# Splitting four layer-2 loads into 6 KB runs, with the mixer computed in one piece instead of two halves

## The chip, the cores and the metric

The kernel is one program for one core of a Trainium2 chip; the other cores are idle. A core has a matrix engine (PE, with its weight loads shown apart as PEld), a vector engine (DVE), an activation engine (ACT), GpSimd (POOL) and a sync engine (SP), which here only issues transfers. Sixteen DMA engines move data between the chip's memory (HBM) and the core's memory of 128 partitions (SBUF). PE writes its results to a small accumulator memory (PSUM). The metric is the device time in microseconds (us); smaller is better. Every engine runs its own list of instructions in order, and waits on semaphores for the others.

## What is computed

One token passes through two layers of attention over a cache, each followed by a small gated-shift network ("mixer"). All tensors are bf16.

```python
def _A_ref(x, k_cache, v_cache, wq, wo):        # x: 1x1x640; 32 heads of 192; the last 4096 of 32768 cache rows
    q = (x @ wq).reshape(B, Sq, Hq, Dh).transpose(0, 2, 1, 3)
    k, v = k_cache[:, :, Sk - W:, :], v_cache[:, :, Sk - W:, :]
    p = softmax(einsum("bhqd,bhkd->bhqk", q, k) * Dh ** -0.5)
    return einsum("bhqk,bhkd->bhqd", p, v) ... @ wo

def _B_ref(x, w1, w2, w3, w4):                  # one row: every shifted quarter of h is padding, so hs = 0 and x1 = x
    ...
    h2 = gelu(layernorm(x1) @ w3) @ w4          # w3 640x1536, w4 1536x640
    return x1 + h2

x = x + _A_ref(layernorm(x), ...)
x = x + _B_ref(layernorm(x), ...)
x = x + _A_ref(layernorm(x), ...)               # the same weights and caches again
x = x + _B_ref(layernorm(x), ...)
```

With a single row the four shifts of the mixer push the row out and bring zeros in, so `w1` and `w2` have no effect on the result and the kernel does not load them. Each layer reads K and V of 32 heads, 4096 x 192 bf16 = 1.5 MB each, and `wo`; the second layer could reuse the first one's data only as far as SBUF holds it.

## The kernel before

**Memory.** SBUF holds eleven "cells" of 12 KB per partition (`NCELL`, `take`, `give`). Every K, every V, every 960 KB piece of `wo`, most of `w3` and most of `w4` occupies a cell. A cell is popped from the front of the list `free` when the load is written down and appended when its last reader has been written down; a load therefore waits, on SP, for the last reader of the cell's previous content. The activations are kept transposed: 640 values as 128 partitions x 5 columns (`ND` = 5).

**Order of the transfers.** `stream` is one fixed list of all loads of both layers, and SP issues them in that order. A K or V load is a single transfer of 128 partitions x 12,288 contiguous bytes (`load_k` L116, `load_v` L121). Exceptions in `load_v`: the last two heads of a layer come as two transfers of 6,144 bytes per partition each, and of V 3 of layer 2 only the second half is loaded, because the first half is kept in PSUM from layer 1 (`v_words` L438; layer 1 works on its head groups in reverse, so that heads 0 to 6 come last). The transposed K of heads 0 to 6 stay in seven cells from layer 1 to layer 2 (`kept`, `NKEEP`). Layer 2's list begins V 0, V 1, V 2, K 7, the half of V 3, `wo` 0, K 8, V 4, K 9. Their cells come free as follows: V 0's when layer 1's last P V is done, V 1's with the last `wo` piece (L480), V 2's with `w4` (L750), K 7's, V 3's, `wo` 0's, K 8's, V 4's and K 9's when PE has read the kept K of heads 0, 2, 3, 4, 5 and 6 (L370; the cell of head 1 becomes the area for transposed K).

**Attention** (L488). Heads are worked in groups of four. For a K, DVE turns 32x32 blocks (`transpose_quart` L303, L320), PE makes the scores (48 matmuls of a head, L370), ACT the exponentials (L406), PE and DVE the small softmax steps; PV is 32 matmuls of a head (`pv`, L457). `out_proj` (L473) multiplies a group's result with its piece of `wo`, 30 matmuls into `y_ps`; `add_y` adds it to the residual. In the last group `add_y` with n = 0 makes two sums: `x1`, and `z`, the same minus a mean that `center_y` took from the partial sum one group earlier. DVE and ACT add up `z` and its square, so that the mixer's layernorm can start from two sums at once.

**Mixer** (L686). Two one-column matmuls against a matrix of ones spread the sums over the partitions (L692, L694). DVE makes the centred input `xc` (L698) and five small steps for the variance (L703 to L710); ACT takes its logarithm and exponential (`power`, L291). PE multiplies `w3` with `xc` in two halves of six columns (60 matmuls, L722). For each half ACT and DVE evaluate gelu from a square, an exponential and reciprocals (L728 to L741); then 60 matmuls with `w4` (L750), in the order of the halves: 30 that need only the first half's gelu, 30 for the second. Written this way the first half's gelu lies beside the `w3` matmuls of the second half, and the second half's gelu beside the first 30 `w4` matmuls. The end adds the residual (L755, L757), and after the second mixer the result is transposed in bf16 (L771), copied and stored (L774).

The engines PE, DVE, ACT and SP follow the order in which the program is written.

Of the kernel before, what the change touches and what calls it, by code (L numbers as in the profile page):

```python
# [33 lines left out]
def kernel(  # L34
# [39 lines left out]
    VKEEP, VHALF = 3, FREE // 2  # L74

# [39 lines left out]

    def load_k(layer, h):  # L116
        t = take(("k", layer, h))
        nc.sync.dma_start(t[:], A_k_cache[0, h, s0:Sk, :].rearrange("(p j) d -> p (j d)", p=P))
        return t

    def load_v(layer, h):  # L121
        t = take(("v", layer, h))
        src = A_v_cache[0, h, s0:Sk, :].rearrange("(p j) d -> p (j d)", p=P)
        n = 2 if h in GROUPS[layer][-1][-2:] else 1
        step = FREE // n
        if (layer, h) == (1, VKEEP):
            n, step = 2, VHALF
        for i in range(n):
            if (layer, h, i) != (1, VKEEP, 0):
                nc.sync.dma_start(t[:, i * step:(i + 1) * step], src[:, i * step:(i + 1) * step])  # L130
        return t
# [5 lines left out]
    def load_wo(layer, c):  # L137
        t = take(("wo", layer, c))
        src = A_wo[c * QC:(c + 1) * QC, :].rearrange("(p c) n -> p (c n)", c=NA)
        n = 2 if c == GROUPS[layer][-1][0] // QH else 1  # L140
        step = NA * D // n
        for i in range(n):
            nc.sync.dma_start(t[:, i * step:(i + 1) * step], src[:, i * step:(i + 1) * step])
        return t
# [112 lines left out]
    nc.vector.memset(eps1[:], eps)  # L257
    Qblk = const.tile([P, H * NCOL, NM], BF16, name="Qblk")
# [32 lines left out]
    def power(var, mul, bias, tag):  # L291

        ln_t = sm.tile([P, 1], F32, tag=tag + "_ln")
        nc.scalar.activation(ln_t[:], var, ACTF.Ln, bias=bias, scale=mul)
# [192 lines left out]
    def attention(layer, x_cur, rs_cur, x_new, z_new, rs_new, ss_new):  # L487
# [3 lines left out]
        junk = sm.tile([P, ND], F32, tag="ln_junk")  # L491
# [5 lines left out]
        def softmax_scale():  # L497
            rstd = power(total()[:, 0:1], 1.0 / D, eps1[:], "rstd")
# [16 lines left out]
        def add_y(y_ps, n):  # L515
            y_new = x_new if n == 0 else sm.tile([P, ND], F32, name="y_acc")
            if n == 1:

                rs = sm.tile([P, 1], F32, name="rs_y")
                nc.vector.scalar_tensor_tensor(out=y_new[:], in0=y_ps[:], scalar=1.0, in1=y[0][:],  # L520
                                               op0=ALU.mult, op1=ALU.add, accum_out=rs[:, 0:1])

                def center():
                    nm_ps = psm.tile([P, 1], F32, tag="psm")
                    nc.tensor.matmul(nm_ps[:], lhsT=ones[:], rhs=rs[:, 0:1], start=True, stop=True)
                    ym = sm.tile([P, ND], F32, name="y_m")
                    nc.vector.scalar_tensor_tensor(out=ym[:], in0=nm_ps[:, 0:1].broadcast_to([P, ND]),
                                                   scalar=-1.0 / D, in1=y_new[:], op0=ALU.mult, op1=ALU.add)
                    y.append(ym)

                y.append(center)
            else:
                if n == 0:
                    nc.vector.scalar_tensor_tensor(out=z_new[:], in0=y_ps[:], scalar=1.0, in1=y[1][:],
                                                   op0=ALU.mult, op1=ALU.add, accum_out=rs_new[:, 0:1])
                    nc.scalar.activation(junk[:], z_new[:], ACTF.Square, accum_out=ss_new[:, 0:1])
                nc.vector.tensor_add(y_new[:], y[0][:], y_ps[:])  # L537
            y[0] = y_new

        def center_y():  # L540
            y.pop()()
# [26 lines left out]
        for gi, cur in enumerate(groups):  # L568
            nxt = list(enumerate(groups[gi + 1])) if gi + 1 < len(groups) else []
            ST_n = None  # L570
            if nxt:
# [23 lines left out]
                else:  # L595
# [24 lines left out]
                    if pending is not None:  # L620
                        add_y(y_ps, 2)
                        pending = None
# [6 lines left out]
            else:  # L629
                if layer == 0:  # L630
                    add_y(out_proj(layer, *pending), 1)
# [5 lines left out]
            for hq, h in enumerate(cur):  # L637
                o_sb = pv(layer, h, hq, PT, fold)
                if final:
                    if layer == 0 and hq == 1:  # L640
                        center_y()
# [32 lines left out]
            if final:  # L674
                if layer == 1:
                    y_ps = out_proj(layer, *pending)
                    fold()
                    add_y(y_ps, 1)
                    center_y()
                else:  # L680
                    fold()
            pending = (cur[0] // QH, oT)
            ST = ST_n
        add_y(out_proj(layer, *pending), 0)

    def mixer(layer, x_cur, z, rs_cur, ss_cur, x_new, rs_new):  # L686

# [3 lines left out]
        s1_ps = psm.tile([P, 1], F32, tag="psm")  # L691
        nc.tensor.matmul(s1_ps[:], lhsT=ones[:], rhs=rs_cur[:, 0:1], start=True, stop=True)  # L692
        s2_ps = psm.tile([P, 1], F32, tag="psm")
        nc.tensor.matmul(s2_ps[:], lhsT=ones[:], rhs=ss_cur[:, 0:1], start=True, stop=True)  # L694
        xc = sm.tile([P, ND], BF16, name="xc")
        xcf = sm.tile([P, ND], F32, name="xcf")
        for t in (xc, xcf):
            nc.vector.scalar_tensor_tensor(out=t[:], in0=s1_ps[:, 0:1].broadcast_to([P, ND]), scalar=-1.0 / D,  # L698
                                           in1=z[:], op0=ALU.mult, op1=ALU.add)

        st = sm.tile([P, 4], F32, name="st")
        m2, s2d, b1, b2 = (st[:, i:i + 1] for i in range(4))
        nc.vector.tensor_scalar(out=b1, in0=s1_ps[:], scalar1=1.0 / D, scalar2=None, op0=ALU.mult)  # L703
        nc.vector.tensor_tensor(out=m2, in0=b1, in1=b1, op=ALU.mult)
        nc.vector.tensor_scalar(out=b2, in0=m2, scalar1=-(1.0 + eps), scalar2=eps * eps, op0=ALU.mult, op1=ALU.add)
        nc.vector.scalar_tensor_tensor(out=s2d, in0=s2_ps[:], scalar=1.0 / D, in1=m2, op0=ALU.mult, op1=ALU.max)
        rr = power(s2d, 1.0 + eps, b2, "rr")
        rg = sm.tile([P, 1], F32, name="rg")
        nc.vector.tensor_scalar(out=rg[:], in0=rr[:], scalar1=GELU_A * GELU_C, scalar2=None, op0=ALU.mult)
        nc.vector.tensor_scalar(out=b1, in0=m2, scalar1=-1.0, scalar2=eps, op0=ALU.mult, op1=ALU.add)  # L710

        HF = NF // 2
        hT = sm.tile([P, NF], BF16, name="hT")
        h_ps = []
        for half in range(2):
            hp = psS.tile([P, 4, NGK, NM], F32, name="ST_ps")
            hp = hp[:, 0].rearrange("p g m -> p (g m)")[:, 0:HF]
            for i in range(HF):
                fc = half * HF + i
                f0 = 2 * P * (fc // 2) + fc % 2  # L720
                for kc in range(ND):
                    nc.tensor.matmul(  # L722
                        hp[:, i:i + 1], lhsT=w3[kc][:, f0:f0 + 2 * P - 1:2], rhs=xc[:, kc:kc + 1],
                        start=(kc == 0), stop=(kc == ND - 1))
            h_ps.append(hp)
        for half, hp in enumerate(h_ps):
            sq = sm.tile([P, HF], F32, name="sq")
            nc.scalar.activation(sq[:], hp, ACTF.Square, scale=rr[:, 0:1])  # L728
            gu = sm.tile([P, HF], F32, name="gu")
            nc.vector.scalar_tensor_tensor(out=gu[:], in0=sq[:], scalar=1.0 / GELU_C, in1=hp,  # L730
                                           op0=ALU.add, op1=ALU.mult)
            ge = sm.tile([P, HF], F32, name="ge")
            nc.scalar.activation(ge[:], gu[:], ACTF.Exp, scale=rg[:, 0:1])

            rh = sm.tile([P, HF], F32, name="rh")
            nc.vector.tensor_scalar(out=rh[:], in0=hp, scalar1=rr[:, 0:1], scalar2=None, op0=ALU.mult)
            nc.vector.reciprocal(rh[:], rh[:])
            nc.vector.scalar_tensor_tensor(out=gu[:], in0=ge[:], scalar=1.0, in1=rh[:],
                                           op0=ALU.add, op1=ALU.mult)
            with nc.allow_low_precision(reason="the matmul's operand, bf16 as in the reference"):  # L740
                nc.vector.reciprocal(hT[:, half * HF:(half + 1) * HF], gu[:])  # L741
        rstd = power(s2d, 1.0, b1, "rstd")
# [5 lines left out]
        order = [(n, half * HF + i) for half in range(2) for n in range(ND) for i in range(HF)]  # L748
        for i, (n, fc) in enumerate(order):
            nc.tensor.matmul(  # L750
                y2_ps[:, n:n + 1], lhsT=w4[fc][:, n * P:(n + 1) * P], rhs=hT[:, fc:fc + 1],
                start=(i == 0), stop=(i == len(order) - 1))
# [9 lines left out]
    rs2 = const.tile([P, 1], F32, name="rs2")  # L762
    z = [const.tile([P, ND], F32, name=f"z{i}") for i in range(2)]
    zs = [const.tile([P, 1], F32, name=f"zs{i}") for i in range(4)]
    attention(0, xT, rs0, x1, z[0], zs[0], zs[1])
    mixer(0, x1, z[0], zs[0], zs[1], x2, rs2)
    attention(1, x2, rs2, x3, z[1], zs[2], zs[3])
    mixer(1, x3, z[1], zs[2], zs[3], x4, None)

# [35 lines left out]
```

## Time and profile before

| | us |
|---|---|
| median of three runs (range) | 537.08 (536.6 to 537.44) |
| the profiled execution | 537.44 |
| its span in the profile | 536.3 |
| PE / PEld / DVE / ACT busy | 282.2 / 230.1 / 260.4 / 55.7 |
| packets of the kernel's transfers, share of 16 DMA engines' span | 97.8% |
| last 480 KB piece of `wo` issued to landed | 15.9 |

The profile's span is one execution as the hardware recorded it; what lies around it, 1.1 us, is start and end of the launch. "GB/s" in a row of stages is what all sixteen DMA engines moved; outside the start, the end and one stretch after layer 1 it is about 424. In the chain of work that ended last, 71% of the span are transfers, and a piece called "issue" is time in which an engine waited for nothing that the profile shows. The transfers named "instruction" are the engines' own program code. A matmul on this page is shown with 165 ns and more, but successive ones overlap: 48 score matmuls with their weight loads take 1.37 us.

### The profile page before, as it was taken

The numbers are of one execution on the slowest core, as the hardware profiler recorded it, in microseconds if no ns is written. First come the engines' busy times: TensorE is split into PE (matmuls) and PEld (weight loads), VectorE is DVE, ScalarE is ACT, GpSimd is POOL, SyncE is SP. The second block draws the span as 40 slices with busy tenths as digits, with TensorE's granted clock in tenths as the row PEclk, the third lists the DMA queues.
The fourth block names the chain that finished last, engine by engine and source line by source line (L and its number), as shares of the span: only waits on it lengthen the run. The fifth ranks groups of instructions, "written<-read, shape, count | busy, mean of one in ns | idle before, by whom it ended". The sixth has DMA issues, their size and how long they took to land.

```text
span 536.3 us, 14902 instructions
## 1 busy us (share of the span) xinstructions
PE 282.2 (53%) x6824; PEld 230.1 (43%) x6824; DVE 260.4 (49%) x519; ACT 55.7 (10%) x253; POOL 2.0 (0%) x11
## 2 busy tenths in 40 slices
PE   0046555365363654545545686666364554536555
PEld 0045444253352543434434664554253443425445
DVE  2187546455455555455414137665454653645612
ACT  1001010010100101001202012010010101001021
POOL 1000000000000000000000000000000000000000
PEclk9999999999999999999999996555555555555555
DMA  8999999999999999999999999999999999999993
GB/s 343 432 426 423 418 427 423 423 425 421 423 422 423 421 424 423 423 424 422 399 404 409 355 369 425 422 424 421 427 420 423 424 420 425 425 423 423 424 412 131
DMA packets 23698, 219.48 MB, mean 409 GB/s; under 512 B 2516, under 2 KB 2900, under 8 KB 8148
## 3 DMA queue, kind: packets, MB, share of 16 engines
q1 hardware_dynamic: 23636, 218.54, 97.8%
q8 instruction: 53, 0.87, 0.7%
q14 instruction: 9, 0.07, 0.0%
HBM read 218.53 MB, written 0.00 MB: 407 GB/s over the span
## 4 chain that ended last, share of the span: by engine, by line
DMA 71%; PE 14%; DVE 12%; issue 2%; ACT 1%; SPq 0%; DVEq 0%
DVE cell_4835 L320 6%; DMA cell_570<-in_A_k_cache_dram 6%; DMA cell_1056<-in_A_k_cache_dram 5%; DMA cell_1668<-in_A_v_cache_dram 5%; DMA cell_2032<-in_A_k_cache_dram 5%; DMA cell_2520<-in_A_k_cache_dram 5%; DMA cell_3009<-in_A_k_cache_dram 5%; DMA cell_7450<-in_A_k_cache_dram 5%; DMA cell_5986<-in_A_k_cache_dram 5%; DMA cell_7943<-in_A_v_cache_dram 5%; DMA cell_6474<-in_A_k_cache_dram 5%; DMA cell_6962<-in_A_k_cache_dram 5%; PE O_ps L457 4%; DMA cell_3469<-in_A_k_cache_dram 4%; PE ST_ps L370 3%; DMA cell_8141<-in_A_wo_dram 3%
## 5 line engine op out<-in xcount | busy, mean ns | idle before, releaser
L370 PE MATMUL ST_ps<-Qblk,cell_203 128*128 128x4 bf16 x1200 | 45.7, 168 | 72.2 <-DVE cell_203 L320 72.2
L370 PE MATMUL ST_ps<-Qblk,cell_4835 128*128 128x4 bf16 x1200 | 45.5, 168 | 64.4 <-DVE cell_4835 L320 63.8
L461 DVE STREAM_TRANSPOSE o_sb<-O_ps 128x192 f32<-128x192 f32 x64 | 24.5, 382 | 112.8 <-PE O_ps L457 112.8
L457 PEld LDWEIGHTS <-PT 128*1 128x1 bf16 x2048 | 68.2, 115 | 22.7 <-issue 11.5
L370 PEld LDWEIGHTS <-cell_203 128*128 128x128 bf16 x1200 | 38.6, 105 | 85.1 <-DVE cell_203 L320 83.4
L370 PEld LDWEIGHTS <-cell_4835 128*128 128x128 bf16 x1200 | 38.6, 105 | 78.1 <-DVE cell_4835 L320 75.3
L470 ACT ACTIVATE oT<-oT_ps,rl 32x6 bf16<-32x6 f32 x64 | 16.5, 257 | 282.4 <-PE oT_ps L469 282.4
L406 ACT ACTIVATE Pr<-ST_ps,nb_sb,sc 128x32 bf16<-128x32 f32 x64 | 25.1, 489 | 0.5
L337 PE MATMUL qT_ps<-xc,wq_sb 128*128 128x1 bf16 x480 | 15.9, 166 | 13.5 <-DMA wq_sb<-in_A_wq_dram 13.0
L469 PE MATMUL oT_ps<-o_sb,Lq 128*32 128x6 f32 x128 | 16.9, 204 | 11.4 <-DVE o_sb L461 11.2
L337 PEld LDWEIGHTS <-wq_sb 128*128 128x128 bf16 x480 | 15.0, 105 | 14.2 <-DMA wq_sb<-in_A_wq_dram 13.7
L469 PEld LDWEIGHTS oT_ps<-o_sb,Lq 128*32 128x32 f32 x128 | 11.9, 141 | 19.8 <-issue 15.3
L415 PEld LDWEIGHTS <-Eq 128*32 128x32 bf16 x256 | 4.0, 105 | 30.9 <-DVE y_acc L537 25.1
L351 PE MATMUL Qrep_ps<-Xq,Lb 128*128 128x24 bf16 (+1 forms) x18 | 3.2, 180 | 24.4 <-DVE Xq L344 24.2
L406 ACT ACTIVATION_READ_ACCUMULATOR Pr<-ST_ps,nb_sb,sc 128x1 f32 x64 | 14.4, 226 | 0.0
L402 ACT COPY nb_sb<-nb_ps 128x4 f32<-128x4 f32 x16 | 2.6, 162 | 113.1 <-PE nb_ps L400 113.1
L344 DVE TENSOR_TENSOR Xq<-qT_ps,maskq 128x24 bf16<-128x24 f32 (+1 forms) x18 | 2.8, 155 | 19.6 <-PE qT_ps L337 19.5
L420 PE MATMUL l_ps<-lpart,ones 128*128 128x4 f32 x32 | 9.5, 366 | 5.3 <-ACT PT L418 5.3
L420 PEld LDWEIGHTS l_ps<-lpart,ones 128*128 128x128 f32 x32 | 8.1, 313 | 6.9 <-ACT PT L418 6.7
L400 PE MATMUL nb_ps<-dg,ones 4*128 4x4 f32 x32 | 9.0, 348 | 1.0
L400 PEld LDWEIGHTS nb_ps<-dg,ones 4*128 4x128 f32 x32 | 7.9, 307 | 1.8
L415 PE MATMUL PT_ps<-Pr,Eq 128*32 128x32 bf16 x256 | 5.3, 192 | 6.0 <-ACT Pr L406 5.8
(285 smaller groups left out, 476.2 us busy)
## 6 DMA issues: line engine op xcount, KB each, us to landing
wq_sb<-in_A_wq_dram SPq DMA_DIRECT2D x5, 1536.0 KB, 11.2
cell_201<-in_A_k_cache_dram SPq DMA_DIRECT2D x1, 1536.0 KB, 21.9
cell_259<-in_A_k_cache_dram SPq DMA_DIRECT2D x1, 1536.0 KB, 25.1
cell_320<-in_A_k_cache_dram SPq DMA_DIRECT2D x1, 1536.0 KB, 25.8
cell_374<-in_A_k_cache_dram SPq DMA_DIRECT2D x1, 1536.0 KB
cell_465<-in_A_k_cache_dram SPq DMA_DIRECT2D x1, 1536.0 KB, 30.3
cell_568<-in_A_v_cache_dram SPq DMA_DIRECT2D x1, 1536.0 KB, 30.3
cell_570<-in_A_k_cache_dram SPq DMA_DIRECT2D x1, 1536.0 KB, 30.3
```

Source lines behind the costliest of these rows:

```text
L320: nc.vector.transpose(Tu, Ku[:, :, q * NY:(q + 1) * NY])
L337: nc.tensor.matmul(qT_ps[:, tl:tl + 1], lhsT=wq_sb[:, kc, t * P:(t + 1) * P], rhs=xc[:, kc:kc + 1], start=(kc == 0), stop=(kc == ND - 1))
L351: nc.tensor.matmul(Qrep_ps[:], lhsT=Lb[:], rhs=held["x"][:].rearrange("p t b -> p (t b)"), start=True, stop=True)
L370: nc.tensor.matmul(ST_ps[:, hq, q * ng + g, :], lhsT=T4[:, g, f, :, t], rhs=Qblk[:, h * NCOL + 2 * f + t, :], start=(n == 0), stop=(n == N ...
L400: nc.tensor.matmul(nb_ps[:], lhsT=ones[0:n, :], rhs=held["dg"][0:n, :], start=True, stop=True)
L406: nc.scalar.activation(out=Pr[:, hq].rearrange("p m g -> p g m"), in_=ST_ps[:, hq], func=ACTF.Exp, bias=nb_sb[:, hq:hq + 1], scale=sc[:, 0 ...
L415: nc.tensor.matmul(PT_ps[32 * m:32 * (m + 1), :, j, :], lhsT=Eq[:, j, :], rhs=held["Pr"][:, :, m, :], start=True, stop=True)
L420: nc.tensor.matmul(l_ps[:], lhsT=ones[:], rhs=held["l"][:], start=True, stop=True)
L457: nc.tensor.matmul(O_ps[r:r + 1, :], lhsT=PT[:, hq, i:i + 1], rhs=V[:, i * Dh:(i + 1) * Dh], start=(i < 4), stop=(i >= NB - 4))
L461: nc.vector.transpose(o_sb[:], O_ps[:].rearrange("p (a c) -> p c a", c=NA))
L469: nc.tensor.matmul(oT_ps[r, :], lhsT=Lq[:], rhs=o_sb[:, :, 0], start=True, stop=True)
L470: nc.scalar.activation(oT[r, :], oT_ps[r, :], ACTF.Copy, scale=rl[r, 0:1])
```

## The change

Two parts are put in place of one another.

Loads: `parts(layer, h)` returns 2 for layer 2 (`layer == 1`) and heads 1, 2 and 7 (`SHORT`), else 1, and `load_k`, `load_v` and `load_wo` issue that many transfers, each over all 128 partitions and 6,144 bytes of each. So V 1, V 2 and K 7 of layer 2 are issued as two transfers each; as the test is on the head's number alone, V 7 is too. K 1 and K 2 are not loaded in layer 2, and `load_wo` asks with multiples of four, which `SHORT` does not hold. Layer 2 issues four transfers more, of the same bytes in total.

Mixer: it works in one piece. `center_y`, `z`, the two sums and the five small variance steps are gone. `add_y` makes the new residual and its row sum; `ln_center`, the function that attention uses already, spreads the mean by one matmul, makes `xc` and `xcf` and sums the squares on ACT; the variance is spread by a matmul (`total`) that stands on PE behind the first 25 of the 60 `w3` matmuls. Gelu runs once on all twelve columns, behind the last `w3` matmul, and `w4` follows it, output column by output column. The result is transposed in bf16, as before.

```diff
+    SHORT = (1, 2, 7)
...
+    def parts(layer, h):
+
+        return 2 if layer == 1 and h in SHORT else 1
+
     def load_k(layer, h):
         t = take(("k", layer, h))
-        nc.sync.dma_start(t[:], A_k_cache[0, h, s0:Sk, :].rearrange("(p j) d -> p (j d)", p=P))
+        src = A_k_cache[0, h, s0:Sk, :].rearrange("(p j) d -> p (j d)", p=P)
+        n = parts(layer, h)
+        step = FREE // n
+        for i in range(n):
+            nc.sync.dma_start(t[:, i * step:(i + 1) * step], src[:, i * step:(i + 1) * step])
...
-        n = 2 if h in GROUPS[layer][-1][-2:] else 1
+        n = 2 if h in GROUPS[layer][-1][-2:] else parts(layer, h)
...
-        n = 2 if c == GROUPS[layer][-1][0] // QH else 1
+        n = 2 if c == GROUPS[layer][-1][0] // QH else parts(layer, c * QH)
...
-            if n == 1:
-                rs = sm.tile([P, 1], F32, name="rs_y")
-                nc.vector.scalar_tensor_tensor(out=y_new[:], in0=y_ps[:], scalar=1.0, in1=y[0][:],
-                                               op0=ALU.mult, op1=ALU.add, accum_out=rs[:, 0:1])
-                def center():
-                    nm_ps = psm.tile([P, 1], F32, tag="psm")
-                    nc.tensor.matmul(nm_ps[:], lhsT=ones[:], rhs=rs[:, 0:1], start=True, stop=True)
...
+        def add_y(y_ps, last):
+            if last:
+                nc.vector.scalar_tensor_tensor(out=x_new[:], in0=y_ps[:], scalar=1.0, in1=y[0][:],
+                                               op0=ALU.mult, op1=ALU.add, accum_out=rs_new[:, 0:1])
+                return
...
+    def mixer(layer, x_cur, rs_cur, x_new, rs_new):
         w3 = need("w3", 0)
-        s1_ps = psm.tile([P, 1], F32, tag="psm")
-        nc.tensor.matmul(s1_ps[:], lhsT=ones[:], rhs=rs_cur[:, 0:1], start=True, stop=True)
-        s2_ps = psm.tile([P, 1], F32, tag="psm")
-        nc.tensor.matmul(s2_ps[:], lhsT=ones[:], rhs=ss_cur[:, 0:1], start=True, stop=True)
...
-        for half in range(2):
-            hp = psS.tile([P, 4, NGK, NM], F32, name="ST_ps")
...
+        xc, xcf, total = ln_center(x_cur, rs_cur)
+        hT_ps = psm.tile([P, NF], F32, tag="psm")
+        for fc in range(NF):
+            f0 = 2 * P * (fc // 2) + fc % 2
+            for kc in range(ND):
+                nc.tensor.matmul(
+                    hT_ps[:, fc:fc + 1], lhsT=w3[kc][:, f0:f0 + 2 * P - 1:2], rhs=xc[:, kc:kc + 1],
+                    start=(kc == 0), stop=(kc == ND - 1))
+            if fc == NF // 3:
+                var_ps = total()
+                rr = power(var_ps, 1.0 + eps, eps2, "rr")
...
+        nc.scalar.activation(sq[:], hT_ps[:], ACTF.Square, scale=rr[:, 0:1])
...
+        nc.scalar.activation(ge[:], gu[:], ACTF.Exp, scale=rg[:, 0:1])
...
+            nc.vector.reciprocal(hT[:], gu[:])
...
-        order = [(n, half * HF + i) for half in range(2) for n in range(ND) for i in range(HF)]
...
+        for n in range(ND):
+            for fc in range(NF):
+                nc.tensor.matmul(
+                    y2_ps[:, n:n + 1], lhsT=w4[fc][:, n * P:(n + 1) * P], rhs=hT[:, fc:fc + 1],
+                    start=(fc == 0), stop=(fc == NF - 1))
```

## The prediction, made before the run

> **What bounds the kernel.** The page comes first: which engine is full, and what the chain that ended last is made of.
>
> ```profile
> PE 282.2 (53%) x6824; PEld 230.1 (43%) x6824; DVE 260.4 (49%) x519; ACT 55.7 (10%) x253; POOL 2.0 (0%) x11
> ...
> q1 hardware_dynamic: 23636, 218.54, 97.8%
> q8 instruction: 53, 0.87, 0.7%
> ...
> DMA 71%; PE 14%; DVE 12%; issue 2%; ACT 1%; SPq 0%; DVEq 0%
> ```
>
> No engine is full; the transfers are. 218.5 MB at 424 GB/s are 515 us of 536.3. A change can save only where the transfers are not at that rate, and at the end, after the last of them. Rows by stage find these places (times, busy us with counts, granted clock, DMA share, GB/s last):
>
> ```profile
> 286.00:299.00 13.00, 8.45 (x228) 8.06 (x229) 4.29 (x31) 2.76 (x13) 0.00 (x0) 1.00 1.03 415
> 299.00:316.00 17.00, 13.70 (x421) 12.62 (x418) 2.26 (x13) 2.47 (x12) 0.00 (x0) 1.00 0.89 326
> 316.00:358.00 42.00, 27.64 (x670) 22.26 (x671) 27.41 (x47) 5.45 (x26) 0.00 (x0) 0.63 1.01 424
> 358.00:511.00 153.00, 80.07 (x1920) 64.75 (x1918) 80.65 (x139) 14.52 (x67) 0.00 (x0) 0.50 1.01 423
> ```
>
> From 299 to 316, the start of layer 2, the rate is 326: 17 x (1 - 326/424) = 3.9 us of transfer time are lost. The timeline of SP shows why: a load goes out only when its cell is free.
>
> ```profile
> 288.17 0.33 SPq L130 DMA_DIRECT2D cell_4829<-in_A_v_cache_dram  x1
> 293.52 0.33 SPq L130 DMA_DIRECT2D cell_4831<-in_A_v_cache_dram  x1
> 299.45 0.33 SPq L118 DMA_DIRECT2D cell_4833<-in_A_k_cache_dram  x1
> 304.39 0.33 SPq L130 DMA_DIRECT2D cell_4962<-in_A_v_cache_dram  x1
> 307.82 0.33 SPq L143 DMA_DIRECT2D cell_5008<-in_A_wo_dram  x1
> 309.11 0.33 SPq L118 DMA_DIRECT2D cell_5010<-in_A_k_cache_dram  x1
> ```
>
> These are V 1, V 2, K 7, half of V 3, `wo` 0 and K 8, freed by PE. What holds PE there is in the chain in order of time:
>
> ```profile
> 293.52 1.86 issue
> 295.38 0.23 PE y_ps L750 x2
> ...
> 300.59 0.99 issue
> 301.58 0.27 PE ST_ps L370 x4
> ...
> 305.53 1.97 issue
> 307.50 1.58 PE ST_ps L370 x53
> ```
>
> Three times PE stands still with nothing to wait for: 4.8 us. I counted PE's instructions up to each stop: 6,849, 7,105 and 7,361, 256 apart. The 53 packets of the queue "instruction" have 16,384 bytes each; PE has 13,705 instructions, so a packet is a block of 256. PE runs out of program. The packet records say when a block came: fetches start at 293.00, 299.10 and 305.17, move for 1.0 us, and PE goes on 1.3 to 1.4 us after their ends. All through the trace a fetch starts after PE has entered the block before it. From that entry to its start it takes 1.9 to 3.7 us in most of the span, about 3.0, while 12,288-byte packets (median 462 ns) fill the engines; at the three stops 5.2, 3.7 and 3.6. Two started with mostly 6,144-byte packets around them (236 ns): 0.9 us at 272.98 and 1.4 at 308.87; one with the queues nearly empty, 0.6 at 529.85. I read it so: the fetch waits behind data packets, and shorter packets shorten the wait.
>
> **The change, part by part.** The sum is made against the profiled 537.44, which is 0.36 above the median of the runs.
>
> *Mixer, second layer: all on the path, after the last transfer.* Before, the first `w3` matmul starts at 528.70 and the last `w4` matmul ends at 533.35: 4.65 us. After: 60 `w3` matmuls 1.74 (528.70 to 530.44); the variance matmul between them 0.45 (distance of the two spreading matmuls); gelu once, from its square to the first `w4` matmul 1.37 as in the first half at 290.37 to 291.74, and 0.05 to reach ACT; 60 `w4` matmuls 1.75. Sum 5.36: +0.7. From below +0.25, if the variance matmul hides; from above +1.05, as in the second mixer DVE waited another 0.33 before L738. What precedes `xc` is as long as before (one vector step, one spreading matmul). I take +0.75. `rr` is no bound: the variance is there 25 x 0.029 + 0.6 = 1.3 us after the first matmul, its logarithm and exponential take 0.55, and `w3` ends at 2.2.
>
> *Mixer, first layer.* The same arithmetic puts the last `w4` matmul near 294.6 instead of 293.5. But the block boundary (6,849) now falls just behind that matmul, since the program before it is nearly equally long: PE computes on to the end of `w4` while the block is fetched. The fetch began at 293.00, behind V 0, which is not split; so the block comes at 295.38 as before, and the next layer's mean matmul starts at about 295.4 instead of 295.86. The 1.1 us is hidden by that wait; without the wait it would be +1.1. V 2 goes out 0.9 us later, at 294.4; V 1 keeps the engines until 296.7, so it is not missed. What queues behind V 2 on SP, K 7, waits for PE until 299 anyway.
>
> *Split loads, the rate.* 16 x 236 ns instead of 8 x 462 per engine are +0.08 us a transfer; by the means (242, 468) +0.13. Four transfers: +0.3 to +0.5; I take +0.45. Four more issues of 0.33 us on SP lie in its waits of several us between the issues shown; were that cover gone, +1.3.
>
> Does a smaller transfer cost more in itself? Layer 2's last V heads go in halves of 768 KB, and the row for 514 to 516, mostly theirs, has 419 GB/s:
>
> ```profile
> 514.00:516.00 2.00, 1.51 (x42) 1.17 (x34) 0.38 (x1) 0.26 (x1) 0.00 (x0) 0.50 1.02 419
> 502.00:508.00 6.00, 4.05 (x93) 3.03 (x97) 2.86 (x6) 0.51 (x2) 0.00 (x0) 0.50 1.00 420
> ```
>
> The Trainium skill speaks against the change here: "DMA: Bandwidth & Descriptors", section "Rules for kernel authors", asks for 1 MiB per transfer or more, and its section on the anatomy of one DMA, told for GpSimd's path, has a fixed 2.0 us for each; by that, four more would be an estimated +8 us and the kernel near 543. The rows show this cost overlapped while others are queued.
>
> *Split loads, the fetches.* Fetch 2 is asked for at 295.4, with V 1's second half and V 2 in the engines, fetch 3 with V 2 and K 7. Wait with 6 KB runs: from below 0.9, from above 3.7 as it was; nearest are the two rows with 6,144-byte packets; as those engines were less full I take 2.0. Then fetch 2 starts at 297.4, its block is there at 299.8, and PE needs it at 300.4 - 0.45 = 299.95: the second stop is gone. Fetch 3: 299.95 + 2.0 + 2.4 = 304.35, needed at 303.7: 0.6 instead of 2.0. The next, at 308.7 against 308.5, may cost 0.2. So PE is ahead by 0.45, then 1.5, then 3.1 us. V 3 goes out at 302.8, `wo` 0 at 304.7, K 8 at 306.0.
>
> The Trainium skill, same page, section "Queues, rings and completion order", has an engine drain a packet of some 9 to 17 descriptors of one ring before it turns to another. By it a fetch would wait for up to 8 x 0.462 = 3.7 us, and 1.9 with 6 KB runs; the 5.2 us at the first stop is beyond that.
>
> *What the transfers gain.* A first packet follows its issue by about 1.05 us here. Taking the engines as one server at 424 GB/s (3.7 us for 1.5 MB), before: V 2 done 300.4, K 7 starts 300.95, is done 304.65, V 3 starts 305.6, is done 307.45, `wo` starts 309.0, V 4 is done 318.7: 3.05 idle. After: K 7 (issued 299.0) starts 300.4, and nothing is idle behind it; V 4 is done 3.0 earlier. From above: the 3.9 us of the stage row, less 0.5 that remains. From below 0, if PE gains nothing; a loss is excluded here, since a shorter packet ahead gives a fetch no longer wait. I take 3.0. From 316 the rate is 424 and the queue stays deep (14 to 30 us from issue to landing), so what is gained there arrives at the end. Late next is nothing until 358, where PE waits for transfers again.
>
> Sum: -3.0 + 0.45 + 0.75 = -1.8; 535.6 against the profiled execution, 535.3 against the median.
>
> **Rivals.**
>
> *Fetches do not shorten (slower).* If the wait is set by something else than run length, fetch 2 takes 3.7 us from 295.38 again, the block comes at 301.5 as before, and the 0.45 is lost too. Gain 0, +0.45 + 0.75: 538.3. For it: only two rows with 6 KB, and the engines were not full in either. Against: the wait follows what is in the engines, from 0.6 to 5.2. It decides from where fetches 2 and 3 together save less than 0.75 us of their 7.3.
>
> *Part of the gain.* One stop stays, because the third fetch falls behind a skewed engine or V 3 and `wo` are short of a full queue anyway: a gain of 1.5 to 2 is 536.3 to 536.8. The engines do end their transfers up to 3 us apart.
>
> *More.* V 1's halves also shorten the first fetch (its record starts when V 0's 128 packets have just been started, so V 0 seems to set it). At 291.5 the first stop is gone, the mean matmul starts at 295.0, and with 3.9 recovered the sum is -2.7 to -3.2: 534.2.
>
> **How the numbers follow.** A measurement of this kernel tells 0.2%, 1.1 us, from no change: faster is below 536.0, slower above 538.2. The forecast, with its own range of 534.4 (gain 3.4, tail +0.25) to 536.2 (gain 2.4, tail +1.05): 0.60, of which 0.06 lies above 536.0. Part of the gain: 0.14, of which 0.02 is faster. More: 0.10. No shortening: 0.16; 538.3 is just beyond the bound, and a longer tail puts it further, so 0.11 is slower. Faster 0.54 + 0.02 + 0.10 = 0.66; same 0.06 + 0.12 + 0.05 = 0.23; slower 0.11. The range leaves out some of "more" and most of "no shortening", 0.2 in all: 533.9 to 537.6.
>
> **What will show it.** In the chain of the changed kernel, between the end of layer 1 and 320 us: an "issue" piece of some 0.5 us right before the mean matmul (L284), none or one under 0.7 at the scores. PE's 6,849th instruction stays at about 295.4. `wo` 0 of layer 2 issued near 304.7. The stage 299 to 316 above 380 GB/s. From the last `wo` matmul to the store +0.75 us. The prediction is wrong if the stops stand as they were, if the stage's rate rises and a later stage's falls by as much, or if the rate of the split transfers themselves is under 400.

## The result

The changed kernel takes 540.97 us (median; 540.07 to 541.9) against 537.26 us on the same measure: 1.007 times the time before, with a 95% interval of 1.0049 to 1.0091. It is slower, by 0.7%. A second comparison on another occasion, below, gave 1.0046 (1.0030 to 1.0062). The ratios here are those on record; they are formed from all the executions and differ a little from the ratio of the two medians. The forecast was 535.3 and faster; the range ended at 537.6.

The profiled execution after has a span of 538.9 us, 2.6 more than before. The chain of work that ended last, in order of time, around the start of layer 2 (start, duration, what):

```profile
293.50 1.75 PE y_ps L712 x60
295.28 0.18 DVE x_138 L719 x2
295.46 0.57 issue
296.03 0.57 PE mean_ps L284 x2
...
300.76 1.44 issue
302.19 0.22 PE ST_ps L381 x3
...
306.12 2.27 issue
308.39 1.53 PE ST_ps L381 x52
```

The first stop is as foretold, a piece of half a microsecond right before the mean matmul. The second and the third, which were to vanish and to shrink to 0.6, are 1.44 and 2.27 us; before they were 0.99 and 1.97. SP's issues show what follows from that (a pair is now one line, x2):

```profile
288.61 0.81 SPq L139 DMA_DIRECT2D cell_4803<-in_A_v_cache_dram  x2
295.19 0.80 SPq L139 DMA_DIRECT2D cell_4806<-in_A_v_cache_dram  x2
299.59 1.65 SPq L127 DMA_DIRECT2D cell_4809<-in_A_k_cache_dram  x2
304.95 0.33 SPq L139 DMA_DIRECT2D cell_4939<-in_A_v_cache_dram  x1
308.67 0.33 SPq L152 DMA_DIRECT2D cell_4985<-in_A_wo_dram  x1
309.95 0.33 SPq L127 DMA_DIRECT2D cell_4987<-in_A_k_cache_dram  x1
```

`wo` 0 goes out at 308.67, not at 304.7, and the stage of 299 to 316 us keeps the rate that it had (times, busy us with counts, granted clock, DMA share, GB/s last):

```profile
286.00:299.00 13.00, 8.56 (x235) 7.83 (x224) 2.85 (x20) 2.25 (x11) 0.00 (x0) 1.00 1.00 390
299.00:316.00 17.00, 13.01 (x414) 12.43 (x415) 2.38 (x12) 2.47 (x12) 0.00 (x0) 1.00 0.91 326
```

The end, from the last piece of `wo` to the transposed result, is the chain's last part:

```profile
512.45 16.23 DMA cell_8114<-in_A_wo_dram
528.68 0.05 issue
...
530.39 0.80 PE hT_ps L680 x25
531.20 0.43 PE var_ps L297 x2
531.62 0.95 PE hT_ps L680 x35
...
532.65 0.28 ACT sq L689
...
534.21 1.75 PE y_ps L712 x60
...
536.20 0.28 PE row_ps L731
```

In the kernel before, the same part of the chain begins and ends so:

```profile
511.04 15.91 DMA cell_8141<-in_A_wo_dram
...
533.60 0.28 PE row_ps L771
```

From the landing at 528.68 to the transposing matmul at 536.20 it is 7.52 us; before it was 526.95 to 533.60, 6.65. That is +0.9. The rest of the 2.6 us is already there when `wo` lands: 528.68 against 526.95, 1.7 us late. Much of this came about where nothing was changed. Two long stretches in which the transfers alone set the time, one of them in layer 1, ran at 423 GB/s before:

```profile
20.00:250.00 230.00, 119.28 (x2896) 97.35 (x2896) 124.88 (x213) 20.91 (x97) 0.00 (x0) 1.00 1.01 423
340.00:500.00 160.00, 84.83 (x2059) 69.19 (x2060) 87.11 (x147) 15.14 (x70) 0.00 (x0) 0.50 1.01 423
```

and after:

```profile
20.00:250.00 230.00, 119.11 (x2896) 97.27 (x2896) 124.50 (x213) 20.91 (x97) 0.00 (x0) 1.00 1.01 422
340.00:500.00 160.00, 85.05 (x2067) 69.08 (x2056) 86.36 (x147) 15.16 (x70) 0.00 (x0) 1.00 1.01 422
```

The records of the single packets resolve this better. From 20 to 250 us a 12,288-byte packet took 465.6 ns in the mean before and 467.2 after. By the starts of the packets, the way from 4 to 118 MB took 271.65 us before and 272.23 after, that from 136 to 216 MB 190.22 and 190.77: +1.1 us together. No step of the prediction has this. Between the two, around the start of layer 2, the way from 118 to 136 MB took 46.95 and 47.64, +0.7; but from one profiled execution to another it lay anywhere between 45.9 and 48.5 with the old mixer and between 46.9 and 48.0 with the new one, so nothing follows from that difference.

### The profile page after: what moved, and what is told of

Same layout as the page of the kernel before. It is cut to its first block, busy times and chain, and to the rows that moved or that the text cites. A ratio compares the mean times of both kernels' runs of the same rounds, so it can differ in the third digit from the quotient of the medians.

```text
span 538.9 us, 14872 instructions
## 1 busy us (share of the span) xinstructions
PE 281.8 (52%) x6820; PEld 229.0 (42%) x6820; DVE 257.4 (48%) x494; ACT 54.7 (10%) x249; POOL 2.0 (0%) x11
## 4 chain that ended last, share of the span: by engine, by line
DMA 70%; PE 15%; DVE 11%; issue 2%; ACT 1%; SPq 0%; DVEq 0%; ACTq 0%
DVE cell_4812 L331 6%; DMA cell_567<-in_A_k_cache_dram 6%; DMA cell_1665<-in_A_v_cache_dram 5%; DMA cell_1053<-in_A_k_cache_dram 5%; DMA cell_2029<-in_A_k_cache_dram 5%; DMA cell_2517<-in_A_k_cache_dram 5%; DMA cell_3006<-in_A_k_cache_dram 5%; DMA cell_7428<-in_A_k_cache_dram 5%; DMA cell_7921<-in_A_v_cache_dram 5%; DMA cell_5964<-in_A_k_cache_dram 5%; DMA cell_6940<-in_A_k_cache_dram 5%; DMA cell_6452<-in_A_k_cache_dram 5%; PE O_ps L468 4%; DMA cell_3466<-in_A_k_cache_dram 4%; PE ST_ps L381 3%; DMA cell_8114<-in_A_wo_dram 3%
```

## Experiments

### Which of the two parts

The load part alone on the kernel before (`load_k` and `load_v` with it, as in the change):

```diff
+    SHORT = (1, 2, 7)
...
+    def parts(layer, h):
+
+        return 2 if layer == 1 and h in SHORT else 1
```

> Only the loads are split; the mixer stays in halves. Theory A (the mixer in one piece costs the time, the split nothing but slightly slower packets): within +0.2 to +0.7 us of the kernel before. Theory B (the split costs most of the 3.7 us): +2 us or more. Both expect the three issue stops of PE at the start of layer 2 as long as before, 4.5 to 5.5 us together, since in the changed kernel the waits of the program fetches did not shorten; had run length mattered, they would be under 2 us together and the time 534 to 535.

The mixer part alone (the changed kernel with no load split):

```diff
-    SHORT = (1, 2, 7)
+    SHORT = ()
```

> Only the mixer is in one piece; no load of layer 2 is split but those that were before. Theory A: +2 to +3.2 us, made of about +0.9 at the end (last wo piece landed to the store) and of V 2 issued 1.2 us or more later behind w4, so that the rate of the stage 286 to 299 falls from 415 to about 390 GB/s. Theory B: +0.9 at the end and at most +0.3 elsewhere, about +1.1 in all.

The changed kernel as it is, on the same measure:

> The changed kernel once more, on the chip of the other three, as the sum that the two parts have to make: +2.6 to +4.5 us against the kernel before. If the parts add up, it is split_only plus mixer_only within 0.7 us.

Measured against 538.77 us for the kernel before: the split alone 538.19, ratio 0.9992 (0.9977 to 1.0006); the mixer alone 540.38, 1.0042 (1.0027 to 1.0057); both 540.84, 1.0046 (1.0030 to 1.0062). The whole loss comes with the kernel that has the new mixer; the split neither gains nor costs anything that can be measured. The tail, from the landing of `wo`'s last piece to the transposing matmul, is 7.52 or 7.53 us in all five profiled kernels with the mixer in one piece and 6.63 to 6.67 in the nine with halves and no split load. In the two with halves and split loads it is 6.29 and 6.30, as the wait of 0.33 us that DVE had before L738 is missing there; why, no run shows.

### What sets a program fetch's wait

Layer 2's V 0 takes the other of two free cells, so that it is issued later:

```diff
+        if (layer, h) == (1, 0):
+            free[0], free[1] = free[1], free[0]
```

> The kernel before, but V 0 and V 1 of layer 2 change cells: V 0 now waits for the last wo piece's cell, and is issued near 288.2 instead of 286.0, after PE has asked for its next block of program (287.8); V 1 follows at once. Theory Q (a fetch waits for what was issued before it): the fetch that began at 293.0 begins at 289.5 to 291.5 when w4's rest is done, the first stop of 1.9 us is gone or under 0.5, K 7 goes out 1.4 to 1.9 us earlier (near 297.8), and the time falls by 0.8 to 1.8 us, to 535.5 to 536.5. Theory R (a fetch waits some fixed time whenever the engines are full, whatever was issued before it): it begins at 292 to 293.5, the stop stays at 1.3 us or more, the time is within 0.5 us of before, or slower by up to 0.5 since V 0 starts late.

The dose of the split doubled, to runs of 3 KB (against the run with the split alone, so with the mixer in halves):

```diff
-        return 2 if layer == 1 and h in SHORT else 1
+        return 4 if layer == 1 and h in SHORT else 1
```

> The kernel before with V 1, V 2 and K 7 of layer 2 issued as four transfers of 3 KB runs each, in place of one of 12 KB. It doubles the dose of the split. If the length of the runs ahead of a program fetch sets its wait (the prediction's step on the fetches), the waits of the 26th to 28th fetch fall from 5.2, 3.7 and 3.6 us to about 1 to 1.5 and the stops of 0.99 and 1.97 us go. If the bytes ahead set it, as the half-sized transfers and the run with a quarter of V 1 and V 2 speak for, the waits stay at 3.5 to 5 us and the stops stand. The time: unchanged, or up to 0.8 us longer, since 3,072-byte packets took 121 ns, which is 484 for 12 KB against 466, over 7.1 MB.

Fewer bytes instead of shorter runs:

```diff
+        if layer == 1 and h in (1, 2):
+            n, step = 1, FREE // 4
...
+        k = (lambda i: i % 8) if layer == 1 and h in (1, 2) else (lambda i: i)
...
-            nc.tensor.matmul(O_ps[r:r + 1, :], lhsT=PT[:, hq, i:i + 1], rhs=V[:, i * Dh:(i + 1) * Dh],
+            nc.tensor.matmul(O_ps[r:r + 1, :], lhsT=PT[:, hq, i:i + 1], rhs=V[:, k(i) * Dh:(k(i) + 1) * Dh],
```

> The kernel before, but of V 1 and V 2 of layer 2 only the first quarter is loaded and used over and over (three quarters of their sums over the cache are left out): 2.4 MB less, 5.6 us of transfer less. It shows what the second program fetch of the mixer's stretch waits for, asked for at 295.4. Theory Q (it waits for data in the engines): these are nearly empty by then, it starts within 1.5 us instead of 3.7, and the second stop of 1.0 us is gone. Theory R (the wait is the fetch's own): it starts 3 us or more after it was asked for and the stop stays. Theory Q also expects the third stop of 2.0 us to shrink, as only K 7 is then under way; the time falls by 5.6 us at most, less where the queue is empty anyway.

From the packet records of the program's queue: the time from PE's entry into a block to the start of the fetch of the next one, for the 26th, 27th and 28th fetch (those behind the three stops).

| kernel | runs of V 1, V 2, K 7 | waits, us |
|---|---|---|
| before | 12 KB | 5.2, 3.7, 3.6 |
| V 0 late | 12 KB | 5.2, 3.7, 4.0 |
| mixer alone | 12 KB | 3.5, 3.9, 3.8 |
| split alone | 6 KB | 5.0, 3.8, 4.2 |
| changed kernel | 6 KB | 5.1, 3.9, 3.7 |
| changed kernel again | 6 KB | 3.5, 3.5, 3.7 |
| split in four | 3 KB | 5.3, 3.7, 3.8 |
| a quarter of V 1 and V 2 | 12 KB of K 7; V 1 and V 2 3 KB | 5.1, 1.1, 2.9 |

The stops in the chain of the kernel split in four:

```profile
293.51 2.18 issue
...
300.90 0.99 issue
...
305.84 2.25 issue
```

and in the chain of the one with a quarter of V 1 and V 2, where the second stop is gone:

```profile
293.49 1.91 issue
...
304.39 1.19 issue
```

In this last one the stage before the missing stop moved only 276 GB/s:

```profile
286.00:299.00 13.00, 8.42 (x228) 8.01 (x229) 4.26 (x31) 2.76 (x13) 0.00 (x0) 1.00 0.73 276
```

A fourfold cut of the run length left the second and third wait at 3.7 and 3.8, so the length of the runs does not set the wait. A cut of the bytes brought the second to 1.1, so the data beside a fetch do have a part in it.

The two rows with short packets, from which the prediction took its 2.0 us, were not of one kind. By the packet records of the kernel before, the engines were busy for 61% of the time in which the fetch of 308.87 waited; they were running empty. But while the fetch of 272.98 waited they were busy for 96%, with packets of 6,144 and 3,072 bytes, and that fetch waited only 0.5 to 1.1 us in all sixteen profiles, with the engines at 89% or more. So full engines alone do not make a wait long, and less full ones do not always make it short: in the changed kernel's second profile they were 84% busy during the second wait, and it was 3.5 us. What sets the wait stays open. The trace of the kernel before held two more rows on run length: the fetch that started at 510.98 waited 2.9 us, with 6,144-byte packets for 29% of the engines' busy time, and the one that started at 522.05 waited 3.1 with full engines and no packet over 7,680 bytes around it. Neither is clearly shorter than the usual 3.0.

The Trainium skill, "DMA: Bandwidth & Descriptors", section "Queues, rings and completion order", has an engine drain a packet of some 9 to 17 descriptors before it turns to another ring; by that, as an estimate, a fetch would have waited half as long behind 6 KB runs and a quarter as long behind 3 KB, which is not what was measured.

The times: V 0 late 538.13 against 538.77 (0.9994, 0.9977 to 1.0011), split in four 538.21 against 538.42 (0.9999, 0.9985 to 1.0012); the quarter 535.44 in a single run, with 2.4 MB less to load. With V 0 issued at 288.47, after the fetch had been asked for at 288.14, the first fetch waited 5.2 us all the same; so it does not wait only for what was issued ahead of it. Whether V 0 sets that wait, as the prediction had supposed, is not settled by this: before and with V 0 late, 123 and 107 packets of 12,288 bytes started between the asking and the fetch. Why the first wait is 5.1 in some executions and 3.5 in others, of the changed kernel too, stays open.

### Where the slower packets come from

What differs between the two kernels in layer 1, up to its last head groups, is the place of the cells. The constants lie ahead of them in SBUF, each small tile taking 32 bytes. The new mixer has six of them fewer (z0, z1, zs0 to zs3) and three more (eps2, rs1, rs3), so the cells begin at byte 89,568 instead of 89,664. A cell is 12,288 bytes, 48 x 256, so all eleven cells have the same place relative to 256 bytes. The first three runs moved them by widening or joining constants.

The kernel before with its cells at 89,696:

```diff
-    eps1 = const.tile([P, 1], F32, name="eps1")
+    eps1 = const.tile([P, 16], F32, name="eps1")[:, 0:1]
```

> The kernel before with one constant made 32 bytes larger, so that all eleven cells begin 32 bytes later: at 89,696 instead of 89,664 bytes of each partition, no longer a multiple of 64, as in the changed kernel (89,568). Nothing else differs. Theory C (the cells' place makes every packet slower): the median 12,288-byte packet takes 464 ns instead of 462, and the time rises by 0.6 to 1.6 us. Theory D (the slower packets of the changed kernel come from the chip or the day): 462 ns, time within 0.4 us of before.

The changed kernel with its cells at 89,600, a multiple of 512:

```diff
-    eps2 = const.tile([P, 1], F32, name="eps2")
+    eps2 = const.tile([P, 16], F32, name="eps2")[:, 0:1]
```

> The changed kernel with one constant made 32 bytes larger, so that the cells begin at 89,600, a multiple of 64 again. Theory C: the packets take 462 ns again and 0.6 to 1.6 us of the changed kernel's loss are gone, so +0.8 to +1.9 us against the kernel before; what stays is the tail of the mixer in one piece, +0.9 to +1.2 between the last wo piece's landing and the store. Theory D: as the changed kernel, +2.1 to +3.7.

The kernel before with its cells at 89,600:

```diff
-    even = const.tile([P, 1], F32, name="even")
+    evlo = const.tile([P, 2], F32, name="evlo")
+    even, lo = evlo[:, 0:1], evlo[:, 1:2]
...
-    lo = const.tile([P, 1], F32, name="lo")
...
-    maskq = const.tile([P, 4], F32, name="maskq")
+    mb = const.tile([P, 8], F32, name="mb")
+    maskq, blkm = mb[:, 0:4], mb[:, 4:8]
...
-    blkm = const.tile([P, NM], F32, name="blkm")
```

> The kernel before with four small constants merged into two, so that the cells begin at 89,600, a multiple of 512, instead of 89,664, a multiple of 64 alone. Theory C1 (only the 64 matters): within 0.4 us of the kernel before, packets 462 ns. Theory C2 (a wider alignment gives more): 460 ns or less and 0.5 us or more faster.

Against 538.43 us: the kernel before moved by 32 bytes 537.64 (0.9987, 0.9974 to 1.0000), so 32 bytes as such do no harm; the changed kernel at 89,600 533.85 (0.9919, 0.9895 to 0.9943); the kernel before at 89,600 **532.81 (0.9897, 0.9876 to 0.9918)**, faster than both kernels by 1%. The medians of the last two differ by 1.04 us, about the tail's 0.9.

Then the places of the two kernels were exchanged:

The kernel before at 89,568, with the joined constants of the run before and two more:

```diff
-    zs = [const.tile([P, 1], F32, name=f"zs{i}") for i in range(4)]
+    zz = const.tile([P, 2], F32, name="zz")
+    zs = [zz[:, 0:1], zz[:, 1:2]] + [const.tile([P, 1], F32, name=f"zs{i}") for i in (2, 3)]
```

> The kernel before with 96 bytes of constants fewer ahead of the cells (even and lo in one tile, maskq and blkm in one, zs0 and zs1 in one), so that the cells start at byte 89,568, where the changed kernel has them, in place of 89,664. Nothing else is changed. Theory P (the place of the cells is the part of the loss that the tail does not explain): the 12,288-byte packets take 467.2 ns in the mean as in the changed kernel, in place of 465.6, and the time is about 1.0 us above the kernel before (ratio 1.001 to 1.003). Theory M (something in the new mixer itself slows the packets, such as its constants' or its operations' use of SBUF): the packets stay at 465.6 ns and the ratio is 1.000.

The changed kernel at 89,664:

```diff
-    eps2 = const.tile([P, 1], F32, name="eps2")
+    eps2 = const.tile([P, 32], F32, name="eps2")[:, 0:1]
...
-        junk = sm.tile([P, ND], F32, tag="ln_junk")
-        ssq = sm.tile([P, 1], F32, tag="ln_ssq")
+        js = sm.tile([P, ND + 1], F32, tag="ln_junk")
+        junk, ssq = js[:, 0:ND], js[:, ND:ND + 1]
```

> The changed kernel with its cells at byte 89,664, where the kernel before has them (eps2 widened to 128 bytes; junk and ssq share a tile to make room). Theory P: the packets take 465.6 ns, and of the loss only the tail's 0.9 us stays: ratio to the kernel before 1.0015 to 1.0025, and about 1 us under the changed kernel as it is. Theory M: packets at 467.2 ns and the ratio 1.004 as the changed kernel had on this measure.

The kernel before at 89,568 took 539.73 against 538.42: 1.0036 (1.0023 to 1.0049). The changed kernel at 89,664 took 539.20: 1.0021 (1.0007 to 1.0034). The rates went with the place and not with the mixer; the kernel before at 89,568:

```profile
20.00:250.00 230.00, 119.11 (x2896) 97.37 (x2896) 124.77 (x213) 20.87 (x97) 0.00 (x0) 1.00 1.01 422
340.00:500.00 160.00, 85.69 (x2081) 69.78 (x2078) 86.21 (x147) 15.39 (x71) 0.00 (x0) 1.00 1.01 422
```

the changed kernel at 89,664:

```profile
20.00:250.00 230.00, 119.02 (x2896) 97.26 (x2896) 124.82 (x213) 20.88 (x97) 0.00 (x0) 1.00 1.01 423
340.00:500.00 160.00, 85.09 (x2063) 69.03 (x2055) 87.32 (x148) 15.13 (x70) 0.00 (x0) 1.00 1.01 423
```

and the kernel before at 89,600:

```profile
20.00:250.00 230.00, 119.50 (x2908) 97.89 (x2909) 126.74 (x216) 20.90 (x97) 0.00 (x0) 1.00 1.01 428
340.00:500.00 160.00, 86.48 (x2105) 70.44 (x2102) 87.70 (x148) 15.42 (x71) 0.00 (x0) 1.00 1.01 427
```

What in the place does it? Three more places, all in the kernel before. At 89,728, 128 above a multiple of 256 (junk and ssq share a tile, as above):

```diff
-    eps1 = const.tile([P, 1], F32, name="eps1")
+    eps1 = const.tile([P, 24], F32, name="eps1")[:, 0:1]
```

> The kernel before with its cells 64 bytes later, at 89,728: a multiple of 128 and not of 256 or 512 (eps1 widened to 96 bytes; junk and ssq share a tile to make room). If any multiple of 128 does what the multiple of 512 did: packets 461.8 ns and a ratio of 0.990. If only 512 (or 256) does: packets at 465 to 467 ns and a ratio of 0.999 to 1.003. The first is a little the likelier.

At 89,344, a multiple of 256 and not of 512 (the joined constants of 89,600, and):

```diff
-    o_fin = const.tile([ND, P], out.dtype, name="o_fin")
+    o_fin = x_bf
```

> The kernel before with its cells at byte 89,344: an odd multiple of 256 bytes, so none of 512 (even and lo share a tile, maskq and blkm share one, and the result is stored from the tile of x). Theory 256: what counts is that a run begins at a multiple of 256; the 12,288-byte packets take 461.8 ns in the mean as at 89,600, and the time is 0.990 of the kernel before. Theory 512: only multiples of 512 are fast; the packets stay at 465 to 467 ns and the ratio at 0.999 to 1.004. I hold the first for the likelier. A sentence by itself: the Trainium skill, "DMA: Bandwidth & Descriptors", section "How a descriptor splits into AXI transactions", tells of pieces of 256 bytes from a 256-byte boundary, which would be the first theory; it counts 384 beats for an aligned run of 12,288 bytes.

At 89,536, 192 above a multiple of 256 (the joined constants of 89,600, and):

```diff
-    zs = [const.tile([P, 1], F32, name=f"zs{i}") for i in range(4)]
+    zz = const.tile([P, 3], F32, name="zz")
+    zs = [zz[:, i:i + 1] for i in range(3)] + [const.tile([P, 1], F32, name="zs3")]
```

> The kernel before with its cells at byte 89,536, which is 192 above a multiple of 256 (the constants of before_480 with one more zs in the shared tile). The places tried so far lie 64, 96 and 128 above one (packets 465.3 to 465.6 ns, ratio 0.9987 to 1) and 224 above one (467.2 ns, ratio 1.0036). If the price grows with the length of the piece left over at the end of the run, 192 comes near 224: 466.5 to 467.2 ns and a ratio of 1.001 to 1.0035. If 224 is a case of its own (the only one of the places tried that is an odd multiple of 32 with a first piece of 32 bytes), 192 is like the three others: 465.5 ns and a ratio of 0.999 to 1.0005. I hold the two for equally likely. A sentence by itself: by the page named for the other run the beats would be 386, 387, 388 for 64, 96 and 128, 390 for 192 and 391 for 224, an estimate that speaks for the first.

All places of the kernel before together; the packets are those of 12,288 bytes from 20 to 250 us.

| cells at | above a multiple of 256 | mean packet, ns | time, beside the kernel as it is, us | ratio (95% interval) |
|---|---|---|---|---|
| 89,344 | 0 | 461.7 | 532.09, 539.02 | 0.9881 (0.9858 to 0.9904) |
| 89,600 | 0 | 461.7 | 532.81, 538.43 | 0.9897 (0.9876 to 0.9918) |
| 89,664 (as it is) | 64 | 465.6 | | 1 |
| 89,696 | 96 | 465.3 | 537.64, 538.43 | 0.9987 (0.9974 to 1.0000) |
| 89,728 | 128 | 465.4 | 538.33, 538.42 | 0.9994 (0.9978 to 1.0011) |
| 89,536 | 192 | 465.5 | 537.63, 539.02 | 0.9985 (0.9971 to 0.9999) |
| 89,568 | 224 | 467.2 | 539.73, 538.42 | 1.0036 (1.0023 to 1.0049) |

A multiple of 256 is what counts; 128 is not enough and 512 is not needed. Off it, the way into the block does not matter, but for 224, the one place tried where a run begins with only 32 bytes before the next multiple of 256. The packets show two kinds of step: at 89,600, 99% of them took 460 ns; at 89,664, 53% took 462 and 20% 469; at 89,568, 61% took 464 and 19% 471. The Trainium skill, the page named above, section "How a descriptor splits into AXI transactions", cuts a run at multiples of 256 bytes, with one piece more when it does not begin on one; it tells this of the bytes that are read, and here the place that is written was moved. The boundary agrees with the two fast places. Its counts of beats, 384 when aligned and 386, 387, 388, 390 and 391 for 64, 96, 128, 192 and 224, are an estimate worked out from its rule; they put 192 near 224, and the runs put it with 64. So the rule's boundary is shown here and its price is not.

## Why the prediction was wrong

**Split loads, the fetches: this step failed.** It took the wait behind 6 KB runs as 2.0 us, between the bounds 0.9 and 3.7, nearest to two rows with short packets. The waits measured 3.9 and 3.7, at the upper bound, and with 3 KB runs they were 3.7 and 3.8: shorter packets do not shorten the wait. In one of the two rows the engines were running empty; the other had packets of 6,144 and of 3,072 bytes and full engines, and why its wait is short is open. The prediction noticed that the engines were less full in its rows and still chose the value from run length, and it did not use the rows of 510.98 and 522.05, in which short packets went with waits of 2.9 and 3.1. It was the rival "Fetches do not shorten", given 0.16, that came true for the transfers; its 538.3 still lacks what the place of the cells cost.

**What the transfers gain: -3.0, measured 0.** It hung on the step above. The stage of 299 to 316 stayed at 326 GB/s. (The stage before it had 390 instead of 415, but kernels with the old mixer and all their loads whole had from 378 to 415 there, so nothing follows from that.)

**Split loads, the rate: +0.45, measured nothing.** The split alone was 0.9992 times the time before, with -1.2 to +0.3 us as the interval; this includes the tail that was 0.35 us shorter with it. That a transfer of half the size costs nothing by itself was right, and at 384 KB, four to a load, still was.

**Mixer, second layer: +0.75, measured +0.9.** Right. From the landing of `wo`'s last piece the order of the pieces and their durations are nearly the ones summed up: `w3` with the variance matmul 2.18 (2.19 in the sum), one gelu 1.56 from its square to the first `w4` matmul (1.37), `w4` 1.75.

**Mixer, first layer: right for this execution.** The longer mixer is hidden behind the fetch, and the stop shrinks from 1.86 to 0.57. The last `w4` matmul ended at 295.25 and not near 294.6; 0.4 of that is that everything in this execution was already later at the end of layer 1 (its last PV at 285.57 instead of 285.15). The mean matmul started 0.17 after that of before instead of 0.45 ahead of it. It hides only where the first fetch is late. In three profiles of the old mixer that fetch waited 3.5 or 3.6 us, the first stop was 0.27 or 0.28, and the way from 118 to 136 MB took 45.9 to 46.4 us, against 46.95 to 48.5 in the others that load the same bytes. In two profiles of the new mixer it waited 3.5 as well, and the way was 47.7 and 47.9, no shorter than in the others. As far as these five profiles tell, the mixer in one piece forgoes 1 us or more in such executions; how often they occur is not on record.

**Not in the prediction: the place of the cells.** The diff takes away six 32-byte constants and adds three, and that moved all eleven cells by 96 bytes. It cost 1.3 us by the medians, 1.2 to 2.6 by the interval, in the kernel before with no other change. The prediction counted what each instruction does and did not ask where the tiles lie; its statement that from 316 us the rate is 424 whatever the change was an assumption, and by 0.3% it was false.

The new sum: 0 from the fetches, 0 from the split, +0.9 from the tail, +1.2 to +2.6 from the place, which is +2.1 to +3.5. The two comparisons gave +2.6 to +4.9 and +1.6 to +3.3, the spans of the profiles +2.6. The sum leaves out what the first layer's mixer forgoes when its fetch is early. The exchanged places give the same split from the other side: with the place of the kernel before, the changed kernel keeps a loss of 0.4 to 1.8 us around the tail's 0.9.

## What to carry to other kernels

When a row is the only evidence for a cause, ask what else is different in that row, and look for a row that has the cause without the rest; here two such rows stood in the same trace, and a run with the dose doubled settled it for little. When a change adds or removes any tile, small constants too, compare the addresses of the large buffers behind them before and after. Where a kernel's time is its transfers, begin the buffers that they fill at a multiple of 256 bytes; here that was worth 1.0 to 1.2% of the time, more than everything that the change was about.

## What was unexpected of the hardware

The destination's place in SBUF changes the duration of a 12 KB packet by 0.8 to 1.2% (461.7 to 465.6 and 467.2 ns), in a kernel whose 16 engines are full for 98% of the span. At the stops a program fetch of 16 KB waited 3.5 to 5.3 us in the kernels that load all their bytes, whether the runs beside it are 12, 6 or 3 KB long, and 1.1 where three quarters of two loads were left out; another, near 270 us, waited only 0.5 to 1.1 beside engines that were at least 89% busy. The stops stand at any place of the cells (at 89,600 they were 0.28, 1.25 and 1.98 us).
